# First k in groups of 16 tiles with sums in matmuls of 512, and q's last products one group ahead of the sums

## The chip, the cores and the metric

One core of a Trainium2 chip. The metric is the device time of one execution in microseconds (us), slowest core; here there is only one. In the views PE is TensorE, PEld its weight loads, DVE VectorE, ACT ScalarE and POOL GpSimd; L150 is a line of kernel.py. The kernel before and the changed kernel each ran six times, alternating on the same chip.

"Single records" are the entries of the trace file that the views sum up.

## The reference, cut to what matters

```
B, N, C = 4, 6016, 256
qn = q / (norm(q, over N) + 1e-6);  kn = k / (norm(k, over N) + 1e-6)
a  = softmax(kn^T @ qn / tau)                 # 256 x 256 for each of 4 batches
x  = (v @ a).reshape(B * N, C)
out = (silu(x @ w_gate) * (x @ w_val)) @ w_out
```

The kernel folds a into w_gate and w_val, so that the loop multiplies v by the folded weights. Only the first batch's attention part stands at the start with nothing to hide it; those of the later batches run beside the loop. The change touches the first batch alone.

## The kernel before: the parts concerned

```python
def first_row_sums(b, t, which, sq, t_last):          # sums of squares over tokens, for k (1) and q (0)
    if t == 0:
        ss_new = psum_gv.tile([P, C], FP32, tag="gv"[which])
        state[b, "ss", which] = ss_new
    pm = pairs[t][1]
    for s in range(pm):
        nc.tensor.matmul(state[b, "ss", which], ones_bf, sq[:, s, :], ...)

# in first_softmax, after the column sums:
    rs = psum_m.tile([P, CH], FP32, tag="misc")
    keep_warm(1)                       # a matmul whose result nobody reads
    row_eps(rs)
    transpose_first_v()                # PE needs v's first tile here
    keep_warm(2)
    for h in range(CH):
        evacuate_first_v(h)            # VectorE, in front of the inverse row sum
    ...                                # exponentials on ScalarE
    row_sum(0)
    wp_matmul(b, 0, 0, units[0], lo); wp_matmul(b, 1, 0, units[1], lo); wp_matmul(b, 2, 0, units[2], lo)
    row_sum(1)
    finish_rs(b, rs)

# loads, all on one queue, in this order: k, q, v's first tile, weights
kgroups = [(s, min(8, NS - s)) for s in range(0, NS, 8)]
...                                    # qgroups of 8, 8, 8, 8, 4, 4, 4, 2, 1 tiles
load_first_v()
load_w(0, HW)
```

Of the kernel before, what the change touches and what calls it, by code (L numbers as in the profile page):

```python
# [8 lines left out]
FP32 = mybir.dt.float32  # L9
# [10 lines left out]
def kernel(  # L20
# [11 lines left out]
    nc = tc.nc  # L32
    P = 128

    B, N, C = q.shape
# [4 lines left out]
    NS = N // P  # L40
# [63 lines left out]
    state = {}  # L104
# [54 lines left out]
    def gemm1_pair(b, t):  # L159

        q_sb, k_sb = qk_tiles[b]
        if t == 0:
            kq_new = psum_kq.tile([P, CH, C], FP32, tag="kq")
            state[b, "kq"] = kq_new
        kq = state[b, "kq"]
        ps, pm = pairs[t]
        last = t == NP - 1
        for jh in range(CH):
            js = slice(jh * P, (jh + 1) * P)
            if pm == 2:  # L170
                nc.tensor.matmul(kq[:, jh, :], q_sb[:, ps:ps + 2, js],  # L171
                                 k_sb[:, ps:ps + 2, :],
                                 start=(t == 0 and jh == 0), stop=last,
                                 perf_mode=DR, skip_group_check=True)
            else:
                nc.tensor.matmul(kq[:, jh, :], q_sb[:, ps, js], k_sb[:, ps, :],  # L176
                                 start=(t == 0 and jh == 0), stop=last,
                                 skip_group_check=True)

    def first_square(b, t, which, on_dve):  # L180
        x_sb = qk_tiles[b][which]
        ps, pm = pairs[t]
        sq = sqpool.tile([P, 2, C], BF16, tag="sq%d" % which)
        if on_dve:
            nc.vector.tensor_mul(sq[:, :pm, :], x_sb[:, ps:ps + pm, :],
                                 x_sb[:, ps:ps + pm, :])
        else:
            nc.scalar.activation(sq[:, :pm, :], x_sb[:, ps:ps + pm, :], ACT.Square)  # L188
        return sq

    def first_row_sums(b, t, which, sq, t_last):

        if t == 0:
            ss_new = psum_gv.tile([P, C], FP32, tag="gv"[which])
            state[b, "ss", which] = ss_new
        pm = pairs[t][1]
        for s in range(pm):
            nc.tensor.matmul(state[b, "ss", which], ones_bf, sq[:, s, :],  # L198
                             start=(t == 0 and s == 0), stop=(t == t_last and s == pm - 1))

    def first_row_copy(b):
        row = work.tile([1, C], FP32, tag="row")
        nc.vector.tensor_copy(row, state[b, "ss", 0][0:1, :])
        state[b, "row"] = row

    def first_cols(b):

        row = state[b, "row"]
        cols = psum_gv.tile([P, CH], FP32, tag="g")
        for h in range(CH):  # L210
            nc.tensor.matmul(cols[:, h:h + 1], row[0:1, h * P:(h + 1) * P],
                             ones_f[0:1, 0:1], start=(h == 0), stop=False,
                             skip_group_check=True)
        state[b, "cols"] = cols

    def first_col_sums(b, t, sq):
        cols = state[b, "cols"]
# [3 lines that stand above are left out]
                nc.tensor.matmul(cols[:, h:h + 1], sq[:, s, h * P:(h + 1) * P],  # L221
                                 ones_bf[:, 0:1], start=False,
                                 stop=(t == NP - 1 and s == pm - 1),
                                 skip_group_check=True)

    def first_root(dst, src):
        nc.scalar.activation(dst, src, ACT.Ln)
        nc.scalar.activation(dst, dst, ACT.Exp, scale=0.5)

    def first_norm_k(b):  # L230
        ink = work.tile([P, C], FP32, tag="ink")
        first_root(ink, state[b, "ss", 1])
        nc.vector.tensor_scalar_add(ink, in0=ink, scalar1=1e-6)
        state[b, "ink"] = ink

# [4 lines left out]
    def first_softmax(b):  # L240
        kq, ink = state[b, "kq"], state[b, "ink"]
        inq = work.tile([P, CH], FP32, tag="inq")
        first_root(inq, state[b, "cols"])
        s_f = work.tile([P, CH, C], FP32, tag="s_f")
        nc.vector.tensor_mul(s_f[:, 0, :], kq[:, 0, :], ink)
        nc.vector.tensor_scalar_add(inq, in0=inq, scalar1=1e-6)
        nc.vector.reciprocal(inq, inq)
        if inv_tau != 1.0:
            nc.vector.tensor_scalar_mul(inq, in0=inq, scalar1=inv_tau)
        nc.vector.tensor_mul(s_f[:, 1, :], kq[:, 1, :], ink)  # L250
        rs = psum_m.tile([P, CH], FP32, tag="misc")
        keep_warm(1)
        row_eps(rs)
        transpose_first_v()
        keep_warm(2)
        for h in range(CH):
            evacuate_first_v(h)
        exT = attn.tile([P, CH, C], BF16, tag="exT")
        state[b, "exT"] = exT
        for jh in range(CH):  # L260
            nc.scalar.activation(exT[:, jh, :], s_f[:, jh, :], ACT.Exp,
                                 scale=inq[:, jh:jh + 1])


        def row_sum(jh):
            for ih in range(CH):
                nc.tensor.matmul(rs[:, ih:ih + 1], exT[:, jh, ih * P:(ih + 1) * P],
                                 ones_bf[:, 0:1], start=False,
                                 stop=(jh == CH - 1), skip_group_check=True)

        units = []
        for u in range(2 * CH):
            unit_ps = psum_gv.tile([P, HW], FP32, tag="gv"[u % 2])
            units.append(unit_ps)
        row_sum(0)
        wp_matmul(b, 0, 0, units[0], lo)
        wp_matmul(b, 1, 0, units[1], lo)
        wp_matmul(b, 2, 0, units[2], lo)
        row_sum(1)
        finish_rs(b, rs)  # L280
        for u, jh in ((0, 1), (1, 1), (2, 1), (3, 0), (3, 1)):
            wp_matmul(b, u, jh, units[u], lo)
        for u in range(4):
            wp_evacuate(b, u, units[u], lo, u % 2 == 1)
        nc.scalar.preload_act_table(ACT.Silu)
        for u in range(2):
            wp_unit(b, u, psum_o, "o", hi, on_dve=True)
# [124 lines left out]
    def keep_warm(n):  # L412
        ps = psum_o.tile([P, 2, C], FP32, tag="o")
        for _ in range(n):
            nc.tensor.matmul(ps, ones_bf, warm_bf, start=True, stop=True)  # L415
# [6 lines left out]
    def wp_matmul(b, u, jh, ps, part):  # L422
        wc, w, ih = wp_units[u]
        cols = slice(wc * WP + part.start, wc * WP + part.stop)
        nc.tensor.matmul(ps, state[b, "exT"][:, jh, ih * P:(ih + 1) * P],  # L425
                         (w_gate_sb, w_val_sb)[w][:, jh, cols],
                         start=(jh == 0), stop=(jh == CH - 1))
# [214 lines left out]



    kgroups = [(s, min(8, NS - s)) for s in range(0, NS, 8)]
    qgroups, at = [], 0
    while at < NS:
        rest = NS - at
# [4 lines left out]
    order = [(g, 1, kgroups) for g in range(NG)] + [(g, 0, qgroups) for g in range(NQ)]  # L653
    for n, (g, which, gl) in enumerate(order):
        load_qk(0, g, which, gl)
        if n == 4:
            make_identity(nc, identf)
            nc.gpsimd.memset(half, 0.5)
            nc.gpsimd.memset(minus, -1.0)
# [8 lines left out]
    G_COLS = NQ - 4  # L668
    T_COLS = qgroups[G_COLS][0] // 2
    for g, which, gl in order:  # L670
        gs, gm = gl[g]
        ts = list(range(gs // 2, (gs + gm + 1) // 2))
        if which == 0 and g == NQ - 1:
            continue
        if which == 0 and g == NQ - 2:

            gs, gm = gl[g + 1]
            ts += range(gs // 2, (gs + gm + 1) // 2)
        if which == 0 and g == G_COLS:
            first_row_copy(0)  # L680
        sqs = [first_square(0, t, which, on_dve=(t % 2 == 1)) for t in ts]
        if which == 0:
            for t in ts:
                gemm1_pair(0, t)
            if g == G_COLS:
                first_cols(0)
            if g == NQ - 4:
                keep_warm(1)
        for t, sq in zip(ts, sqs):
            if which == 0 and g >= G_COLS:  # L690
                first_col_sums(0, t, sq)
            else:
                first_row_sums(0, t, which, sq, (T_COLS if which == 0 else NP) - 1)
        if which == 0:
            if g == 0:
                first_norm_k(0)
                nc.vector.tensor_copy(ident, identf)
            elif g <= 4:
                first_inv_k(0, g - 1)

            if g == G_COLS:
                keep_warm(1)
    first_softmax(0)


# [81 lines left out]
```

## Time and profile before

| | before |
|---|---|
| time, median of the six runs (lowest to highest) | 809.93 us (809.37 to 810.98) |
| span of the profiled execution | 807.6 us |
| PE busy | 787.9 us (98%) |
| q's fourth group: products start | 28.36 us |
| column sums end | 34.45 us |
| PE's v transposes start | 34.93 us |
| first product sv of the loop | 39.63 us |

The loop from about 37.6 us on is bound by PE and is not touched. What counts of the start is therefore one number, the time of the first sv product: whatever moves it moves the end.

### The profile page before, as it was taken

How to read it: one execution, taken by the hardware profiler on the slowest of the kernel's cores; microseconds unless marked ns; L12 is line 12 of the kernel's file. 1: busy time of each engine (PE TensorE's matmuls, PEld its weight loads, DVE VectorE, ACT ScalarE, POOL GpSimd, SP SyncE). 2: the span in 40 equal slices, each digit the busy share in tenths (PEclk: the TensorE clock that was granted, in tenths of full speed). 3: DMA queues.
4: the chain of work that ended last, by engine and by line, in shares of the span. 5: the costliest groups of instructions: out<-in, count | busy, mean ns of one | idle time of the engine just before them, and what ended most of it. 6: DMA issues, size and time to landing. Idle time of an engine off the chain costs nothing.

```text
span 807.6 us, 11833 instructions
## 1 busy us (share of the span) xinstructions
PE 787.9 (98%) x3867; PEld 384.4 (48%) x3940; DVE 554.7 (69%) x854; ACT 454.3 (56%) x802; POOL 251.0 (31%) x302
## 2 busy tenths in 40 slices
PE   4999999999999999999999999999999999999998
PEld 3644444444454444444454444444445444444446
DVE  4777878758667878766766778766866665665654
ACT  4666666555556666555555656555555555555553
POOL 4415887332104786332000777610000000000000
PEclk8999999999999999999999999999999999999999
DMA  9995999799886685887976697667556665565443
GB/s 89 143 154 97 147 190 174 144 142 178 149 145 144 131 153 121 152 137 166 145 170 144 113 160 149 131 126 166 128 116 123 144 134 131 125 149 130 117 113 99
DMA packets 203567, 112.43 MB, mean 139 GB/s; under 512 B 151424, under 2 KB 190337, under 8 KB 202753
## 3 DMA queue, kind: packets, MB, share of 16 engines
q1 hardware_dynamic: 185456, 84.55, 44.1%
q0 software_dynamic: 17904, 27.01, 30.6%
q8 instruction: 31, 0.51, 0.3%
q14 instruction: 32, 0.25, 0.1%
q10 hardware_dynamic: 144, 0.10, 0.0%
HBM read 79.06 MB, written 60.48 MB: 173 GB/s over the span
## 4 chain that ended last, share of the span: by engine, by line
PE 95%; DMA 3%; issue 1%; ACT 0%; DVE 0%; POOL 0%; ACTq 0%; POOLq 0%
PE g_ps L458 30%; PE v_ps L458 30%; PE o_new L499 29%; PE ps L425 2%; DMA q_sb<-in_q_dram 2%; PE kq_new L171 2%; PE o_new L552 1%; DMA k_sb<-in_k_dram 1%; ACT silu L464 0%; DVE sv L468 0%; PE ss_new L198 0%; PE last_ps L576 0%; PE unit_ps L425 0%; PE kq_new L176 0%; PE ps L415 0%
## 5 line engine op out<-in xcount | busy, mean ns | idle before, releaser
L468 DVE TENSOR_TENSOR sv<-silu,v_ps 128x512 bf16<-128x512 bf16 (+1 forms) x576 | 386.5, 673 | 214.5 <-ACT silu L464 213.1
L464 ACT ACTIVATE silu<-g_ps 128x512 bf16<-128x512 f32 (+1 forms) x576 | 339.1, 589 | 292.5 <-PE g_ps L458 263.7
L458 PE MATMUL g_ps<-vT,Wg 128*128 128x512 bf16 (+1 forms) x1109 | 326.5, 375 | 1.2
L458 PE MATMUL v_ps<-vT,Wv 128*128 128x512 bf16 (+1 forms) x1104 | 325.1, 374 | 1.0
L499 PE MATMUL o_new<-sv,w_out_sb 128*128 128x512 bf16 (+1 forms) x1079 | 319.1, 375 | 1.4
L458 PEld LDWEIGHTS <-Wv 128*128 128x128 bf16 x1152 | 112.7, 98 | 130.9 <-ACT Wv L437 0.4
L303 POOL TENSOR_TENSOR acc_new<-acc_new,sq 128x512 f32<-128x512 f32 x135 | 157.2, 1165 | 52.6 <-DVE sq L293 37.3
L458 PEld LDWEIGHTS <-Wg 128*128 128x128 bf16 x1152 | 111.3, 98 | 125.8 <-DVE Wv L435 0.2
L499 PEld LDWEIGHTS <-w_out_sb 128*128 128x128 bf16 x1104 | 108.0, 98 | 126.5
L129 POOL DMA_DIRECT2D vb_new<-in_v_dram x47 | 24.2, 516 | 244.9 <-DMA vT<-vb_new 243.8
L509 DVE COPY pl<-o_new 128x512 uint16<-128x512 uint16 (+1 forms) x92 | 62.5, 680 | 14.1 <-ACT pl L508 13.9
L293 DVE TENSOR_TENSOR sq<-q_sb 128x512 bf16<-128x512 fp8e5 x72 | 65.8, 914 | 0.0
L508 ACT COPY pl<-o_new 128x512 uint16<-128x512 uint16 (+1 forms) x92 | 53.1, 578 | 19.8 <-PE o_new L499 19.1
L294 ACT ACTIVATE sq<-k_sb 128x512 bf16<-128x512 fp8e5 x72 | 44.2, 614 | 0.0
L171 PE MATMUL kq_new<-k_sb,q_sb 128*128 128x512 fp8e5 x184 | 28.4, 295 | 1.4 <-DMA q_sb<-in_q_dram 1.3
L114 POOL DMA_DIRECT2D q_sb<-in_q_dram x45 | 25.4, 564 | 11.7 <-DMA k_sb<-in_k_dram 9.8
L198 PE MATMUL ss_new<-sq,ones_bf 128*128 128x256 bf16 x83 | 14.8, 336 | 10.9 <-ACT sq L188 10.9
L171 PEld LDWEIGHTS <-q_sb 128*128 128x256 fp8e5 x184 | 21.2, 137 | 6.3 <-DMA q_sb<-in_q_dram 2.7
L114 POOL DMA_DIRECT2D k_sb<-in_k_dram x42 | 23.2, 554 | 2.9 <-DVE sv L468 1.7
L370 POOL TENSOR_SCALAR den<-th 128x512 f32<-128x512 f32 x3 | 1.8, 614 | 64.4 <-ACT th L369 64.4
L338 POOL TENSOR_TENSOR inv<-inv,half 64x8 f32<-64x8 f32 x3 | 5.0, 1665 | 53.3 <-DVE inv L336 53.3
L298 POOL TENSOR_TENSOR acc_new<-sq 128x512 f32<-128x512 bf16 x3 | 3.5, 1151 | 47.1 <-DVE sq L293 47.1
(90 smaller groups left out, 208.4 us busy)
## 6 DMA issues: line engine op xcount, KB each, us to landing
rows<-pl SPq DMA_DIRECT2D x86, 256.0 KB, 2.6
out_dram<-ot_new SPq DMA_DIRECT2D x43, 512.0 KB, 4.1
vb_new<-in_v_dram POOLq DMA_DIRECT2D x43, 256.0 KB, 4.8
q_sb<-in_q_dram POOLq DMA_DIRECT2D x36, 128.0 KB, 5.9
k_sb<-in_k_dram POOLq DMA_DIRECT2D x33, 128.0 KB, 7.4
ot_new<-rows SPq DMA_TRANSPOSE x92, 3.7
k_sb<-in_k_dram POOLq DMA_DIRECT2D x5, 256.0 KB, 9.0
rows<-pl SPq DMA_DIRECT2D x6, 192.0 KB, 2.4
```

What stands on the lines that cost most here:

```text
L114: nc.gpsimd.dma_start(out=dst[:, gs:gs + gm, :], in_=src[b].rearrange("(p s) c -> p s c", s=NS)[:, gs:gs + gm, :])
L129: nc.gpsimd.dma_start(out=vb[:mv, :].rearrange("(p s) c -> p (s c)", s=cm), in_=v[b, cs * P:cs * P + mv, :].rearrange("(p s) c -> p (s c)" ...
L171: nc.tensor.matmul(kq[:, jh, :], q_sb[:, ps:ps + 2, js], k_sb[:, ps:ps + 2, :], start=(t == 0 and jh == 0), stop=last, perf_mode=DR, skip_ ...
L293: nc.vector.tensor_mul(sq[:, :pm, 0, :], q_sb[:, ps:ps + pm, :], q_sb[:, ps:ps + pm, :])
L294: nc.scalar.activation(sq[:, :pm, 1, :], k_sb[:, ps:ps + pm, :], ACT.Square)
L303: nc.gpsimd.tensor_tensor(out=acc, in0=acc, in1=sq[:, s, :, :], op=ALU.add)
L458: nc.tensor.matmul(dst[:, :mv], W[:, kk, fs], vT[:, kk, :mv], start=(kk == 0), stop=(kk == CH - 1))
L464: nc.scalar.activation(silu[:, :mv], g_ps[:, :mv], ACT.Silu)
L468: nc.vector.tensor_mul(sv[:, f, :mv], silu[:, :mv], v_ps[:, :mv])
L499: nc.tensor.matmul(self.o_ps[h][:, :self.mv], w_out_sb[:, f, h * P:(h + 1) * P], self.sv[:, f, :self.mv], start=(f == 0), stop=(f == FH - 1))
L508: nc.scalar.copy(pl[:, 0, :self.mv], halves[:, 0, :self.mv])
L509: nc.vector.tensor_copy(pl[:, 1, :self.mv], halves[:, 1, :self.mv])
```

## The change: its intent, and the diff

Fewer and larger transfers for k, half as many matmuls for k's sums, reciprocals where VectorE has room, one weight product moved behind the second row sums, and products of q's last groups before the sums of the group ahead of them, so that PE does not wait for squares.

```diff
     def first_row_sums(b, t, which, sq, t_last):
         if t == 0:
-            ss_new = psum_gv.tile([P, C], FP32, tag="gv"[which])
+            ss_new = psum_gv.tile([P, 1 + which, C], FP32, tag="gv"[which])
...
+        if which == 1:
+            nc.tensor.matmul(ss[:, :pm, :], ones_bf, sq[:, :pm, :], start=(t == 0),
+                             stop=(t == t_last), skip_group_check=True)
+            return
...
     def first_norm_k(b):
-        first_root(ink, state[b, "ss", 1])
+        ss = state[b, "ss", 1]
+        nc.vector.tensor_copy(ink, ss[:, 0, :])
+        nc.vector.tensor_add(ink, ink, ss[:, 1, :])
+        first_root(ink, ink)
...
-        wp_matmul(b, 2, 0, units[2], lo)
         row_sum(1)
         finish_rs(b, rs)
-        for u, jh in ((0, 1), (1, 1), (2, 1), (3, 0), (3, 1)):
+        for u, jh in ((0, 1), (1, 1), (2, 0), (2, 1), (3, 0), (3, 1)):
...
-    kgroups = [(s, min(8, NS - s)) for s in range(0, NS, 8)]
+    kgroups = [(s, min(16, NS - s)) for s in range(0, NS, 16)]
...
-            elif g <= 4:
-                first_inv_k(0, g - 1)
+            elif g <= 2:
+                first_inv_k(0, 2 * g - 2)
+                first_inv_k(0, 2 * g - 1)
...
+    first_row_copy(0)
+    waiting = []
+    for n, g in enumerate(range(G_COLS, NQ - 1)):
+        ts = range(qgroups[g][0] // 2, (qgroups[g + 1][0] if n < 2 else NS + 1) // 2)
+        sqs = [(t, first_square(0, t, 0, on_dve=(t % 2 == 1))) for t in ts]
+        for t in ts:
+            gemm1_pair(0, t)
+        if n == 0:
+            first_cols(0)
+            keep_warm(1)
+        for t, sq in waiting:
+            first_col_sums(0, t, sq)
+        waiting = sqs
+    for t, sq in waiting:
+        first_col_sums(0, t, sq)
```

(Cut: the old loop over q's last groups, which had two keep-warm matmuls there; the new inner loop that takes a group's squares four pairs at a time; the index of the row copy; where the identity is made; blanks.)

More of the change, by code (lines that the diff above doesn't have):

```diff
@@ L193, in first_row_sums @@
         if t == 0:
-            ss_new = psum_gv.tile([P, C], FP32, tag="gv"[which])
+            ss_new = psum_gv.tile([P, 1 + which, C], FP32, tag="gv"[which])
             state[b, "ss", which] = ss_new
         pm = pairs[t][1]
+        ss = state[b, "ss", which]
+        if which == 1:
+            nc.tensor.matmul(ss[:, :pm, :], ones_bf, sq[:, :pm, :], start=(t == 0),
+                             stop=(t == t_last), skip_group_check=True)
+            return
         for s in range(pm):
-            nc.tensor.matmul(state[b, "ss", which], ones_bf, sq[:, s, :],
-                             start=(t == 0 and s == 0), stop=(t == t_last and s == pm - 1))
+            nc.tensor.matmul(ss[:, 0, :], ones_bf, sq[:, s, :], start=(t == 0 and s == 0),
+                             stop=(t == t_last and s == pm - 1))
     def first_row_copy(b):
         row = work.tile([1, C], FP32, tag="row")
-        nc.vector.tensor_copy(row, state[b, "ss", 0][0:1, :])
+        nc.vector.tensor_copy(row, state[b, "ss", 0][0:1, 0, :])
         state[b, "row"] = row
@@ L655 @@
         load_qk(0, g, which, gl)
-        if n == 4:
+        if n == 3:
             make_identity(nc, identf)
@@ L670 @@
     for g, which, gl in order:
+        if which == 0 and g >= G_COLS:
+            break
         gs, gm = gl[g]
         ts = list(range(gs // 2, (gs + gm + 1) // 2))
-        if which == 0 and g == NQ - 1:
-            continue
-        if which == 0 and g == NQ - 2:
-            gs, gm = gl[g + 1]
-            ts += range(gs // 2, (gs + gm + 1) // 2)
-        if which == 0 and g == G_COLS:
-            first_row_copy(0)
-        sqs = [first_square(0, t, which, on_dve=(t % 2 == 1)) for t in ts]
-        if which == 0:
-            for t in ts:
-                gemm1_pair(0, t)
-            if g == G_COLS:
-                first_cols(0)
-            if g == NQ - 4:
-                keep_warm(1)
-        for t, sq in zip(ts, sqs):
-            if which == 0 and g >= G_COLS:
-                first_col_sums(0, t, sq)
-            else:
+        for at in range(0, len(ts), 4):
+            now = ts[at:at + 4]
+            sqs = [first_square(0, t, which, on_dve=(t % 2 == 1)) for t in now]
+            if which == 0:
+                for t in now:
+                    gemm1_pair(0, t)
+            for t, sq in zip(now, sqs):
                 first_row_sums(0, t, which, sq, (T_COLS if which == 0 else NP) - 1)
@@ L697 @@
                 nc.vector.tensor_copy(ident, identf)
-            elif g <= 4:
-                first_inv_k(0, g - 1)
-            if g == G_COLS:
-                keep_warm(1)
+            elif g <= 2:
[7 more added lines that the diff above has]
+        for t in ts:
+            gemm1_pair(0, t)
+        if n == 0:
[6 more added lines that the diff above has]
+        first_col_sums(0, t, sq)
     first_softmax(0)
```

## The prediction

> **What bounds the kernel now.** The page first: PE is busy for 98% of the span and the chain that ended last is 95% PE, nearly all of it in the feed-forward loop (three groups of about 30% each), which the diff does not touch.
>
> ```profile
> PE 787.9 (98%) x3867; PEld 384.4 (48%) x3940; DVE 554.7 (69%) x854; ACT 454.3 (56%) x802; POOL 251.0 (31%) x302
> ```
>
> So only the start, before the loop's first product (g_ps at 37.64 us), can change: every group of instructions that the diff names runs before it. I read that start with three views. First the busy time by stretches (columns: window, length, then busy us and count of PE, PE weight loads, DVE, ACT, POOL; granted PE clock; mean DMA share; GB/s written).
>
> ```profile
> 12.00:14.40 2.40, 1.12 (x8) 0.77 (x8) 1.16 (x3) 1.02 (x3) 0.40 (x2) 1.00 1.05 106
> 14.40:17.80 3.40, 2.52 (x12) 1.64 (x12) 2.25 (x4) 1.94 (x4) 0.88 (x2) 0.51 1.06 106
> 17.80:21.30 3.50, 3.18 (x15) 1.88 (x14) 1.37 (x3) 1.49 (x3) 0.60 (x2) 0.50 1.07 107
> 21.30:24.70 3.40, 2.98 (x27) 2.46 (x26) 2.50 (x6) 2.65 (x6) 0.98 (x2) 1.00 1.06 107
> 28.30:31.70 3.40, 3.30 (x28) 2.79 (x28) 3.20 (x7) 2.41 (x4) 1.95 (x3) 1.00 1.11 106
> ```
>
> The DMA share stays above 1 at a flat 106 GB/s written, which is four times that read, since fp32 becomes fp8: up to about 28 us loading is the bound, and PE, DVE and ACT have slack. In the last line it turns: PE 3.30 of 3.40 us, DVE 3.20. The clock was at half from 14.4 to 21.3 us. Second view, the chain in order of time (start, us, what):
>
> ```profile
> 9.24 19.08 DMA q_sb<-in_q_dram
> 28.36 1.09 PE kq_new L171 x8
> 29.44 0.89 PE ss_new L198 x8
> 30.77 0.47 PE ss_new L198 x4
> 31.26 0.42 DVE row L203
> 31.73 0.60 PE cols L211 x4
> 32.83 0.24 PE ps L415
> 33.06 0.44 PE kq_new L171 x4
> 33.50 0.32 PE cols L221 x8
> 34.32 0.13 PE cols L221 x6
> ```
>
> The last transfer that the chain waits for is q's fourth group of 8 tiles, at 28.36 us. After it PE runs almost without a gap: products and sums of groups four and five, a hop over DVE (the row copy), then column sums and products in turn, to 34.45 us and on into the loop. The later q groups land (32.77, 33.4 and 33.76 us by the starts of their squares) before PE gets to them; they are not the bound. Third, VectorE's own timeline there:
>
> ```profile
> 22.86 0.29 DVE L233 TENSOR_SCALAR ink<-ink 128x256 f32<-128x256 f32 x1 [0.61 <-ACT ink L228]
> 23.58 1.29 DVE L185 TENSOR_TENSOR sq<-q_sb 128x512 bf16<-128x512 fp8e5 x2 [0.29 <-DMA q_sb<-in_q_dram]
> 24.79 0.55 DVE L238 RECIPROCAL ink<-ink 128x64 f32<-128x64 f32 x1
> 28.43 1.29 DVE L185 TENSOR_TENSOR sq<-q_sb 128x512 bf16<-128x512 fp8e5 x2 [0.66 <-DMA q_sb<-in_q_dram]
> 30.65 0.54 DVE L238 RECIPROCAL ink<-ink 128x64 f32<-128x64 f32 x1
> ```
>
> Its squares wait for data by 0.3 to 0.7 us per group. That is the slack a delay can eat.
>
> **What the Trainium skill says.** "TensorE: Matmul & The Clock Gate", section "Part 1: The HAM clock gate", has the array at half clock until a free-running activity window of about 3.4 us was busy. The trace agrees: half clock for two such windows (14.4 to 21.3 us), PE 74% and 91% busy in them, and full clock after the second; it had dropped after a window with short bursts. "DMA: Bandwidth & Descriptors", section "Anatomy of one DMA", gives a transfer a fixed cost of some 2 us, mostly completion. In a queue of transfers this does not show: a group of 8 tiles (1.05 MB read) follows the one before in 2.46 us, a group of 4 in 1.255, so the fixed part of one is 2 x 1.255 - 2.46 = 0.05 us. "VectorE: DVE Perf Modes", section "Why PSUM operands drop a tier", keeps fp32 operations on PSUM at one element per cycle; here the multiply of 256 columns out of PSUM takes 0.42 us and the row copy 0.41.
>
> **The change part by part.**
> (a) k in 3 transfers instead of 6. Bytes stay. By the fixed part above 3 x 0.05 = 0.15 us less, so q's fourth group is ready at about 28.2. k's last group, now 15 tiles, still lands at about 18.4, but all at once.
> (b) k's sums: 47 matmuls of 256 columns become 23 of 512 and one of 256. The same columns, so the same PE time: 0.22 us per 256 columns cold (1.87 us for 8, less the pipeline's 0.15). Two steps are new: the two halves must be added, a copy and an add out of PSUM, 0.4 us each, 0.8 in all on DVE, in front of the root on ACT (0.36 + 0.42).
> (c) What arrives at once is worked off late. 8 pairs are squared by ACT and DVE at 0.58 and 0.61 us each: 18.45 + 4 x 0.61 = 20.9, where the last pairs of before were squared by 19.6. If PE is cold, its 7.5 pairs of 0.43 us run from 19.05 to 22.3 and hold the four square buffers. Then q's first group on DVE (1.21), copy and add (0.8), root on ACT (0.8), add and cast (0.4).
>  Warm: q's first squares on DVE 20.85 to 22.1, copy and add to 22.9, root to 23.75, then to 24.2. Cold: 0.55 later, 24.75. Before it was 23.3.
> (d) The four reciprocals (0.47 each from start to start) move to q's second and third groups, two each. DVE then needs 1.21 + 0.94 = 2.15 us per group of 2.46. Warm: second group 24.2 to 26.35, third to 28.5, and the fourth group's squares start at 28.5, 0.07 later than before. Cold: 29.05, 0.6 later; as PE reaches the last sum of that group only at 30.1, about 0.3 of it gets through.
> (e) No reciprocal stands before the row copy any more: nothing on the path, as the copy waited for PE's sums (31.23).
> (f) Products one group ahead: PE now does cols, one keep-warm matmul, products of group six, sums of five, products of the rest, sums of six and the rest. The same instructions but for one keep-warm matmul of 512 columns: 0.22 to 0.24 us off a stretch where PE is the bound. The wait for squares that the order is to hide hardly existed: the gaps of PE in that stretch sum to 0.16 us and the chain calls them issue.
> (g) The third weight product goes behind the second row sums. These start up to 0.1 us earlier, the inverse row sum too; but PE does all eight products before the loop in any case. Credit 0.05.
> Sum, warm: -0.15 - 0.23 - 0.05 + 0.07 = -0.36 us. Cold: -0.43 + 0.3 = -0.1.
>
> **The rivals.** First, a backlog on a cold PE. k's third burst and q's first group at half clock are 3.25 + 8 x 0.22 + 8 x 0.22 = 6.8 us of PE from 19.05. The full clock comes when a window was busy, which the phase of the window decides: between 22.5 and 26 us. At 26 q's first group is done at 25.9, three groups of 1.75 follow, then the fifth's 0.9: the row copy at about 32.0 instead of 31.26, so +0.75 less the 0.43 gained: +0.3. For it: the array went cold in a stretch of bursts before. Against: continuous cold work is what warms it, and from 22.5 on there is 0.7 us of slack per group.
> Second, the instruction fetch. One fetch of 16 KB on its own queue lies at 30.6 us (945 ns on one of the 16 DMA engines) and holds up q's last three groups by 0.5 us. PE has 48 rows fewer (7824 against 7872) before the loop, so the same fetch comes after q's end, near 33 us. It would make q's end earlier by 0.5 us, but PE gets to those groups at 33.06, 33.82 and 34.09, after they are ready. Worth 0, and at most 0.1. The first v tile, that the fetch may hit instead, is wanted at about 34.8 and lands at 34.5 on the slow DMA engine even now.
> Third, that DVE's extra 0.8 us gets through whole, which gives +0.2 net. The idle time before its squares speaks against it.
>
> **Range and chances.** A gain of 0.1 to 0.4 in most phases and a loss of up to 0.3 in some, mean about -0.15: 809.5. The runs of before lie from 809.41 to 810.98, wider than the effect, so the range is set by that spread and by the phase: 808.6 to 810.8. Two per cent would be 16 us, half of the whole start; the change cannot reach it either way.
>
> **What would show it.** Right: the loop's first g_ps within 0.5 us of 37.64; k's last squares end near 20.9; two operations of about 0.4 us on DVE before the root; the fourth q group's squares start at 28.3 to 29.1; PE without gaps from about 28.3; the fetch after 32.5 us; one keep-warm matmul between cols and the softmax. Wrong: a gap of PE after 29 us, a row copy later than 31.9, a first transfer that starts later than 2.6 us or runs slower per byte with rows twice as long, or loop time that differs at all (then it is noise or alignment, not this change).

## The result, and the profile after

| | before | after |
|---|---|---|
| time, median of six (lowest to highest) | 809.93 (809.37 to 810.98) | 809.84 (809.48 to 810.24) |
| span of the profiled execution | 807.6 | 808.0 |

The ratio is 0.9998, with a 95% interval of 0.9985 to 1.0011. It is the mean time of the changed kernel's fast runs over that of the fast runs of before in the same rounds, so not quite the ratio of the two medians. The times say: no difference that six runs can see; the interval alone is 2.1 us wide (0.0026 x 810).

The traces see more, because the loop repeats itself: the products sv of the two traces, taken in order, differ by 0.17 us at the first and by 0.20 or 0.21 us at each one looked at from the 25th to the last (800.08 against 800.29). So a shift at the start can be read to some hundredths of a us, but in one execution of each kernel only. (The two profiled runs took 809.42 and 809.76 us. The spans of the six runs after lie from 807.7 to 808.5, so two single spans say nothing.)

| moment (us) | before | after | difference |
|---|---|---|---|
| q's fourth group: products start | 28.36 | 28.23 | -0.13 |
| row copy starts | 31.26 | 31.13 | -0.13 |
| column sums end (start + length of the last group) | 34.45 | 34.12 | -0.33 |
| v's first tile landed (single records) | 34.88 | 35.32 | +0.44 |
| v's transposes on PE start | 34.93 | 35.37 | +0.44 |
| first row sums of the exponentials | 35.90 | 36.26 | +0.36 |
| second row sums | 36.36 | 36.53 | +0.17 |
| first sv product | 39.63 | 39.80 | +0.17 |

Down to the column sums the change gained 0.33 us. Then, within one step, 0.77 us were lost. The timeline of PE around that step shows it (start, length, engine, line, operation; in brackets the idle time before it and what ended it). Before:

```profile
34.16 0.29 PE L221 MATMUL cols<-ones_bf,sq 128*128 128x1 bf16 x6
34.62 0.38 PE L389 MATMUL rs<-eps,ones_f 1*128 1x2 f32 x2
34.93 0.62 PE L150 MATMUL vt_ps<-ident,v_sb 128*128 128x128 bf16 x8
35.90 0.20 PE L267 MATMUL rs<-ones_bf,exT 128*128 128x1 bf16 x2
36.36 0.19 PE L267 MATMUL rs<-ones_bf,exT 128*128 128x1 bf16 x2
```

After:

```profile
33.49 0.63 PE L227 MATMUL cols<-ones_bf,sq 128*128 128x1 bf16 x14
34.29 0.38 PE L397 MATMUL rs<-eps,ones_f 1*128 1x2 f32 x2
35.37 0.62 PE L150 MATMUL vt_ps<-ident,v_sb 128*128 128x128 bf16 x8 [0.70 <-DMA v_sb<-in_v_dram]
36.26 0.19 PE L276 MATMUL rs<-ones_bf,exT 128*128 128x1 bf16 x2
36.53 0.19 PE L276 MATMUL rs<-ones_bf,exT 128*128 128x1 bf16 x2
```

PE came to the transposes about 0.33 us earlier and stood idle for 0.70 us, waiting for v's first tile. The view of before shows no such wait, but the single records say that v let go of PE there too. Before, v landed at 34.88 us and PE's first load of it began 45 ns later; after, it landed at 35.32 us and the load began 42 ns later. Eight loads of q that waited for their data began 41 to 43 ns after the landing. So in both kernels, as far as the records tell, the transposes follow v. The 0.44 us by which they moved are those by which v moved, and the 0.33 us gained ahead of them counted for nothing. (The view of before names no wait because it lets the small matmuls ahead, `rs<-eps,ones_f`, run to 35.00 us. How long PE stood there cannot be read.) The list of PE's waits between 30 and 40 us, after, names nothing else (columns: us in total, times, longest):

```profile
PE vt_ps L150 <- DMA v_sb<-in_v_dram: 0.7, 1, 0.7
```

The chain of waits of the changed kernel has turned over with it. Where it ran through q's fourth group, PE's products and the row copy, it now is the v transfer from its issue on (start, us, what):

```profile
23.59 11.73 DMA v_sb<-in_v_dram
35.32 0.05 issue
35.37 0.62 PE vt_ps L150 x8
35.99 0.43 PE ps L423 x2
36.42 0.03 PE rs L276 x2
```

How the lateness reaches the loop is seen on VectorE and ScalarE. Before:

```profile
35.59 0.76 DVE L157 COPY vT_new<-vt_ps 128x512 bf16<-128x512 bf16 x2
36.59 0.17 DVE L407 RECIPROCAL smr<-rs 128x2 f32<-128x2 f32 x1 [0.24 <-PE rs L267]
36.85 0.47 ACT L437 ACTIVATE Wg<-unit_ps,smr 128x256 bf16<-128x256 f32 x1 [0.61 <-PE unit_ps L425]
37.71 1.28 ACT L285 ACT_TABLE_LOAD   x1
39.00 1.08 ACT L464 ACTIVATE silu<-g_ps 128x512 bf16<-128x512 f32 x2
```

After:

```profile
36.03 0.76 DVE L157 COPY vT_new<-vt_ps 128x512 bf16<-128x512 bf16 x2 [0.74 <-PE vt_ps L150]
36.76 0.17 DVE L415 RECIPROCAL smr<-rs 128x2 f32<-128x2 f32 x1
37.02 0.47 ACT L445 ACTIVATE Wg<-unit_ps,smr 128x256 bf16<-128x256 f32 x1 [1.11 <-PE unit_ps L433]
37.88 1.28 ACT L293 ACT_TABLE_LOAD   x1
39.17 1.08 ACT L472 ACTIVATE silu<-g_ps 128x512 bf16<-128x512 f32 x2
```

Before, the inverse row sum (RECIPROCAL smr) waited 0.24 us for PE. After, the view names no wait, because the copies of v's transposes fill VectorE until then. By the single records it follows PE's second row sums in both: they are told done at 36.56 and 36.73 us, and it starts 24 and 23 ns later. After, PE works without a gap from the transposes to these sums, so they are late because v is. From there everything is shifted by 0.17 us: the first weight evacuation, the table load for the silu, the first silu.

Of the 0.44 us at the transposes, 0.27 came back on the way to the second row sums. Before, the first row sums waited for the exponentials: PE was through its last keep-warm matmul at 35.82 us (35.60 + 0.22), and they began at 35.90. And the third weight product, which stood ahead of the second row sums, took 0.11 us, after a wait of 0.07 for its weights (landed at 36.21, product at 36.25). After, none of the three stands there.

**Why v came late, as far as the two traces tell.** v's first tile was issued at 23.74 us before and at 23.59 after, and took 11.14 and 11.73 us to land. Two explanations can be checked against the traces.

That it was queued later or behind more work, or that the larger k groups slowed the queue: no. It was issued 0.15 us earlier, and the last q group in front of it landed earlier (33.00 us against 33.64). A landing is told by 16 records, and the first 15 of v's came earlier too (the 15th at 34.24 us against 34.39). Only the 16th was late. The last square of q, on VectorE, waited for its data before and for something else after:

```profile
33.76 0.43 DVE L185 TENSOR_TENSOR sq<-q_sb 128x256 bf16<-128x256 fp8e5 x1 [0.30 <-DMA q_sb<-in_q_dram]
```

```profile
33.18 0.42 DVE L185 TENSOR_TENSOR sq<-q_sb 128x256 bf16<-128x256 fp8e5 x1 [0.45 <-PE cols L227]
```

That a fetch of PE's instructions got in the way: the records of both kernels fit it, but no run tested it. The first fetch of the program's own instructions after the start is one packet of 16 KB on a queue of its own. The view of the DMA queues (packets, MB, share of 16 engines) finds it between 30 and 32 us before:

```profile
q0 software_dynamic: 274, 0.20, 110.0%
q8 instruction: 1, 0.02, 3.0%
```

and between 33 and 34.5 us after, when v is being read; each kernel has no such packet in the other's window:

```profile
q0 software_dynamic: 406, 0.28, 123.6%
q8 instruction: 1, 0.02, 4.0%
```

By the single records it lies at 30.59 us for 945 ns before, and at 33.17 us for 949 ns after. The place fits PE's program: up to the first column sum the changed kernel has 46 weight loads and matmuls fewer on record (202 against 248), and the fetch starts when PE has begun 232 of them before and 240 after. The landing records show what goes with it:

| how far the 16th landing record is behind the 15th (us) | before | after |
|---|---|---|
| the 12 transfers that landed before the fetch had ended | 0.03 to 0.07 | 0.03 to 0.05 |
| the first transfer that lands after the fetch has ended | 0.56 (q's seventh group) | 1.08 (v's first tile) |
| v's first tile | 0.49 | 1.08 |
| the five transfers after v | 0.48 to 0.57 | 0.8 to 0.9 |

So in each kernel one sixteenth of the transfer falls behind at the fetch and stays behind. In the changed kernel the nine q groups that follow the larger k groups show no such lag; it begins with v. Had v's 16th record come 0.05 us after the 15th in both, v would have landed at about 34.4 us before and 34.3 after (an estimate from these records).

Two coincidences in time are not a test, and it stays open why the lag was 1.08 us after and 0.56 before, with fetches of the same length. Of the 0.44 us by which v's last record moved, 0.20 had come in by the end of its last data packet (34.56 us before, 34.76 after; the last three packets took 233 to 295 ns instead of 173). No record says what the other 0.24 were.

One thing does not hang on this. With v landing at 34.88 us, as before, the transposes could not have begun before 34.93, and the first row sums not before 35.82, where PE came free, instead of 35.90. At most 0.08 of the 0.33 us gained ahead of v could have reached them.

### The profile page after: what moved, and what is told of

The parts are those of the page before. It is cut to its first block, busy times and chain, and to the rows that moved or that the text cites. A ratio compares the mean times of both kernels' runs of the same rounds, so it can differ in the third digit from the quotient of the medians.

```text
span 808.0 us, 11840 instructions
## 1 busy us (share of the span) xinstructions
PE 790.9 (98%) x3916; PEld 381.3 (47%) x3916; DVE 554.1 (69%) x856; ACT 454.3 (56%) x802; POOL 249.3 (31%) x299
## 4 chain that ended last, share of the span: by engine, by line
PE 95%; DMA 4%; POOL 0%; issue 0%; DVE 0%; POOLq 0%
PE g_ps L466 30%; PE v_ps L466 30%; PE o_new L507 29%; PE ps L433 2%; DMA q_sb<-in_q_dram 2%; PE kq_new L171 2%; DMA v_sb<-in_v_dram 1%; PE o_new L560 1%; PE last_ps L584 0%; POOL k_sb L114 0%; PE unit_ps L433 0%; PE kq_new L176 0%; PE vt_ps L150 0%; POOL q_sb L114 0%; PE ps L423 0%
## 5 line engine op out<-in xcount | busy, mean ns | idle before, releaser
L466 PE MATMUL g_ps<-vT,Wg 128*128 128x512 bf16 (+1 forms) x1128 | 330.6, 375 | 0.0
L466 PE MATMUL v_ps<-vT,Wv 128*128 128x512 bf16 (+1 forms) x1128 | 330.4, 374 | 0.0
L507 PE MATMUL o_new<-sv,w_out_sb 128*128 128x512 bf16 (+1 forms) x1104 | 324.5, 376 | 0.0
L114 POOL DMA_DIRECT2D k_sb<-in_k_dram x39 | 21.5, 551 | 1.0 <-POOLq L782 0.8
L200 PE MATMUL ss_new<-sq,ones_bf 128*128 128x512 bf16 (+1 forms) x24 | 9.2, 538 | 12.0 <-ACT sq L188 12.0
```

The costliest lines, as they stand in the source:

```text
L114: nc.gpsimd.dma_start(out=dst[:, gs:gs + gm, :], in_=src[b].rearrange("(p s) c -> p s c", s=NS)[:, gs:gs + gm, :])
L466: nc.tensor.matmul(dst[:, :mv], W[:, kk, fs], vT[:, kk, :mv], start=(kk == 0), stop=(kk == CH - 1))
L507: nc.tensor.matmul(self.o_ps[h][:, :self.mv], w_out_sb[:, f, h * P:(h + 1) * P], self.sv[:, f, :self.mv], start=(f == 0), stop=(f == FH - 1))
```

## The experiments

All were built to move PE's fetch, or to make one part of the change alone. None gave a measurement. Both kernels use the double-row mode for the fp8 products.

**e1_k512**, the kernel before with only k's sums changed (and their two halves added, as in the change).

```diff
+        if which == 1:
+            nc.tensor.matmul(ss[:, :pm, :], ones_bf, sq[:, :pm, :], ...)
+            return
```

> The kernel before with only k's sums as matmuls of 512 (46 PE rows fewer). Theory (instruction fetch hits the first v tile): PE's first instruction fetch of 16 KB moves from 30.6 us to about 33.5 us, holds one DMA engine for about 0.95 us while v's first tile is read, so PE's v transposes start at 35.1 to 35.5 us (before: 34.93) after a wait for v, and the first sv product at 39.6 to 40.0 (before: 39.63). Rival A (the v wait of the changed kernel comes from the larger k groups or the later issue of v): transposes at 34.9, first sv at 39.6, no wait for v. The time stays within 0.1% either way.

**e2_ahead**, the kernel before with only the order of q's last products.

```diff
+        waiting = sqs            # as in the diff of the change, second part
```

> The kernel before with only q's last products one group ahead of the sums (one keep-warm matmul less; PE rows before that unchanged, so the fetch stays near 30.6 us). Theory: the column sums end 0.2 to 0.25 us earlier (34.2 instead of 34.45), but v's first tile, 0.93 us late on one DMA engine, still lands at about 34.85, so the transposes start near 34.9 and the first sv product moves by 0 to -0.1 us. Rival B (PE is the bound through to the loop, as predicted): first sv 0.2 us earlier, 39.4.

**e3_pad48**, the changed kernel with PE's instruction count put back.

```diff
+    pad_ps = psum_m.tile([P, CH], FP32, tag="misc")
+    for _ in range(24):
+        nc.tensor.matmul(pad_ps, ones_bf, warm_bf[:, :CH], start=True, stop=True)
```

> The changed kernel with 24 tiny matmuls (48 PE rows) at its start, where PE idles, so that PE's rows stand as in the kernel before. Theory: the fetch is back at about 30.5 us, v's first tile lands at 34.7 to 34.9 instead of 35.29, the transposes start at 34.7 to 34.9 (changed kernel: 35.37) and the first sv product at 39.2 to 39.5 (39.80). Rival A: transposes at 35.4 and first sv at 39.8 as in the changed kernel.

**e4_q512**, the changed kernel with q's row sums as matmuls of 512 too, so that the fetch comes later, and their halves added by one reduction. (The 34 rows in its expectation are a miscount: q's 36 tiles need 18 matmuls and 18 loads fewer, so 36 rows.)

```diff
-        for s in range(pm):
-            nc.tensor.matmul(ss[:, 0, :], ones_bf, sq[:, s, :], ...)
+        nc.tensor.matmul(ss[:, :pm, :], ones_bf, sq[:, :pm, :], ...)
...
-        nc.vector.tensor_copy(row, state[b, "ss", 0][0:1, 0, :])
+        nc.vector.tensor_reduce(out=row, in_=ss[0:1, :, :].rearrange("p w c -> p c w"),
+                                axis=AX.X, op=ALU.add)
```

> The changed kernel with q's row sums too as matmuls of 512 (34 PE rows fewer), the two halves added by one reduction that is about 0.27 us longer than the row copy and lies on the path. Theory: the fetch comes at 34.0 us or later, after v's first tile has left the queue; v lands near 34.3, the transposes start at 34.5 to 34.9 without a wait for v, first sv at 39.2 to 39.6. Rival A: transposes wait for v until 35.4 and first sv is at 39.8 or later.

The same questions were put to a second family without the mode. There each product of a pair takes its first tile alone, as a plain fp8 matmul, so that the number of PE instructions stays; the result is wrong. It has two controls, **n1_before** and **n2_after**, and the plain forms of e3_pad48 and e4_q512 (**n3_pad48**, **n4_q512**).

```diff
-                nc.tensor.matmul(kq[:, jh, :], q_sb[:, ps:ps + 2, js],
-                                 k_sb[:, ps:ps + 2, :], ..., perf_mode=DR, ...)
+                nc.tensor.matmul(kq[:, jh, :], q_sb[:, ps, js], k_sb[:, ps, :], ...)
```

> Control, wrong result on purpose: the kernel before, with each product of a pair of q and k tiles made of the first tile alone, as a plain matmul without the double-row mode (same number of PE instructions, about the same length). Both theories: the first sv product stays within 0.2 us of 39.63, PE's first fetch of 16 KB near 30.6 us, v's transposes at 34.8 to 35.0.

> Control, wrong result on purpose: the changed kernel with the same plain products. Both theories: first sv within 0.2 us of 39.80, fetch near 33.1 us, transposes at 35.2 to 35.5 after a wait of 0.6 to 0.9 us for v.

No chip ran these. So the theory (the fetch made v later) and its rival (the new grouping or issue order did) were never tested against each other on the chip, and the parts of the change were not measured singly.

## Why the prediction was right or wrong

The time was right: 809.84 us measured against 809.5, inside 808.6 to 810.8, and the same within 2%. That says little for the sum behind it, and in that sense it was luck: the range was set by the spread of the runs, so a sum that is wrong by some tenths falls in it too. In the one pair of traces the sum has the wrong sign: -0.36 us was foretold for the warm branch, which came, and the first sv product moved by +0.17. The six runs neither confirm nor refute the gain of 0.15 us that it put in the middle; the medians differ by 0.09 us.

By its steps, in the traces:

- (a) Fewer transfers, 0.15 us: q's fourth group came 0.13 us earlier. Right. (Its 1.255 us for a group of 4 stands in no view. The two landings there are 1.25 and 1.32 us apart; their mean would make the fixed part 0.11 us. Three transfers fewer gave 0.04 each.)
- (c), (d) The "warm" branch came. k's third burst on PE took 2.10 us for 8 matmuls of 512, where the first and second took 3.57, and VectorE's four squares of it ended at 20.78 us (predicted 20.9). The two extra operations took 0.42 us each (0.4). VectorE's squares of the fourth group began at 28.35 us, 0.08 earlier than before, not 0.07 later. The lines:

```profile
19.12 2.10 PE L200 MATMUL ss_new<-sq,ones_bf 128*128 128x512 bf16 x8 [0.99 <-ACT sq L188]
22.10 0.42 DVE L239 COPY ink<-ss_new 128x256 f32<-128x256 f32 x1
22.55 0.42 DVE L240 TENSOR_TENSOR ink<-ink,ss_new 128x256 f32<-128x256 f32 x1
28.35 1.24 DVE L185 TENSOR_TENSOR sq<-q_sb 128x512 bf16<-128x512 fp8e5 x2
31.13 0.41 DVE L209 COPY row<-ss_new 1x256 f32<-1x256 f32 x1 [0.63 <-PE ss_new L204]
```

  The first rival, a backlog on a cold PE, did not show in this execution, and neither did the third, that VectorE's extra time gets through whole: the row copy waited 0.63 us for PE.
- (f) One keep-warm matmul less, 0.23 us: from the row copy to the end of the column sums 3.19 us before (34.45 - 31.26) and 2.99 after (34.12 - 31.13), 0.20 less. Right. But the wait for squares, which the new order was to hide, was there before and stayed: by the single records PE stood for ScalarE's square from about 33.34 to 33.46 us before and from about 33.69 to 33.82 after. The gap of 0.16 us that the prediction quotes as "issue" is no wait: the first keep-warm matmul falls there, with its weight load at 32.25 us and its own record missing.
- (g) The third weight product behind the second row sums: credited with 0.05 us. These came 0.46 us after the first ones before and 0.27 after (36.36 - 35.90, 36.53 - 36.26): 0.19 less, nearly all of it the product's 0.11 and its wait of 0.07 for weights. So in these traces (g) was put too low; it hid part of what v cost. (Without the earlier exponentials it could have saved only about 0.07: before, the second ones were done at 36.25 us.)
- **The step that failed** is the last sentence of the second rival: that v's first tile "is wanted at about 34.8 and lands at 34.5 on the slow DMA engine even now". 34.5 is the last completion packet in the queue; the landing is on record at 34.88 us, so the slack was not 0.3 us but, as far as the records tell, none: the transposes already followed v. With it fails the statement that PE's work runs "to 34.45 us and on into the loop": the 0.33 us gained on that path ended at v. And v's landing was held fixed, while it came 0.44 us later. The term stands in the sum with 0. At the transposes it was 0.44 us, where -0.33 had been gained, and 0.17 of that reached the loop. Of "a gap of PE after 29 us", which the prediction named as what would show it wrong, the idle 0.70 us is the instance.

The fetch moved to 33.17 us, as foretold ("near 33 us"), and q's end came 0.64 us earlier (foretold 0.5) for no gain, as foretold; what it would hit instead was asked and waved off. Its "7824 against 7872" rows are about those of the whole program, not of the part before the loop (the page counts 3867 matmuls and 3940 loads in all); the difference is what matters.

## What to carry to other kernels

When PE is brought forward, list every transfer that it meets afterwards and compare each landing time, not the last packet, with the new time of need; a transfer that landed just in time is the next bound. A gain shows as such only where the next wait is reached, so read the chain beyond the last touched line. Where a view names no wait, compare the start of an instruction with the landing that it needs: a start 0.04 us after it was a wait here. And changing the number of instructions ahead of a point also moves the fetches of instructions; here one sixteenth of the transfers fell behind at the fetch in both kernels, but no run tested that the fetch was the cause.

## What the Trainium skill lacked or had wrong

- "Runtime: NRT & Kernel Launch", section "Instruction fetch mechanics", has an engine's program fetched in 16 KB blocks over a DMA queue of its own, at a cost that is mostly hidden. The blocks agree with the traces (31 packets of 16 KB before, 30 after). What a fetch can do to loads beside it is not said: at the first one, of 945 and 949 ns, the last of a transfer's 16 landing records fell 0.56 and 1.08 us behind the others. That the fetch caused it was not tested.
- "DMA: Bandwidth & Descriptors", section "Anatomy of one DMA", gives about 2 us fixed per transfer, but not how little of it the next transfer in a full queue feels: three transfers fewer brought q 0.13 us forward, 0.04 each.
